# Sparse value rows fetched by SyncE at register addresses instead of GpSimd's indirect gathers

## The chip, the cores and the metric

The kernel runs on one core of a Trainium2 chip. A core has TensorE (PE in the profile; its weight loads are PEld), VectorE (DVE), ScalarE (ACT), GpSimd (POOL) and SyncE (SP), which each run one list of instructions in order and wait for each other on semaphores. Sixteen DMA engines move data between memory and the core; SP, ACT and POOL can issue transfers to them. The metric is the device time of one execution in microseconds: before the change the median of three runs is 290.01 (289.61 to 290.08).

## The reference

Attention of 4 batches with 8 heads, 768 positions and head dimension 64, with a block-sparse mask of 32 x 32 blocks (24 blocks a side), then a gated feed-forward layer on the 3072 x 512 result:

```python
scores = scale * np.matmul(q, k.transpose(0, 1, 3, 2))
mask = np.abs(blk_i - blk_j) <= 1
mask = mask | (blk_i == 0) | (blk_j == 0) | (blk_i == n_blocks - 1) | (blk_j == n_blocks - 1)
for qb in range(n_blocks):
    for kb in sampled_blocks[qb]:          # three per query block, drawn at random
        mask[qb * block:(qb + 1) * block, kb * block:(kb + 1) * block] = True
scores = np.where(mask, scores, -1000000000.0)
attn = softmax(scores)
x = (attn @ v) as (3072, 512)
rms = np.sqrt(np.mean(x * x, axis=-1, keepdims=True) + 1e-06)
xn = x / rms * rms_g
g = xn @ w_gate
silu = g * (1.0 / (1.0 + np.exp(-g)))
out = (silu * (xn @ w_val)) @ w_out
```

So a query block in the middle sees eight key blocks: its own and its two neighbours, the first, the last, and up to three sampled ones, which can coincide with the others or with each other.

## The kernel before

Batch 0 is computed densely, with the mask added in the score product: three groups of 256 positions (`groups`), eight heads each. While this runs, the kernel prepares the sparse part. Batches 1 to 3 are cut into 18 *chunks* of four query blocks (`chunks`, lines 70 to 75): five regular ones per batch, and one "wide" chunk with blocks 0, 23, 1 and 22, of which the first two see every key. The wide chunks are numbers 5, 11 and 16.

Each key or value block of 32 positions is held as 16 rows, two positions side by side. So the eight blocks that a query block sees fill exactly 128 partitions: three sampled blocks in partitions 0 to 47 (from `R0`), the first block in 48 to 63 (`F0`), the window of three in 64 to 111 (`W0`), the last in 112 to 127 (`L0`).

The values of a batch are cast to bfloat16 (`cast_v`), written to a table in memory (`table`, 384 rows of 1056 elements, that is 2112 bytes, with 16 rows of zeros behind them, `zero_rows`), and fetched from it. `gather_v` (line 508) issues for each query block one indirect transfer on GpSimd that fetches 128 rows of the table by 128 row numbers, a column of `vidx`, into a buffer `vgs[i % 2][:, j, :]`. `vidx` is built once: constant parts by `iotas`, sampled rows by DVE in `index_steps`, which sends a sampled block that repeats another block to the zero rows. There are 66 gathers: four for each of 15 regular chunks, two for each of three wide ones.

The loop over the chunks (line 1078) runs 19 steps of ten positions. In step `i` PE computes the scores of chunk `i` and, at position 0, the values product of chunk `i-1` (`values`, line 634, matmuls of L644), which reads that chunk's buffer. Position 1 and 2 normalise it, 4 squares it on ACT, 5 takes the power on GpSimd, and at position 7 DVE scales it (`x_scaled`, line 688) and SP sends a transposing transfer of it into `xg` (line 700); chunks 4, 8, 16 and 17 are transposed by PE instead (`by_pe`). At position 2, step `i` issues the gathers for chunk `i+1`. The first gathers, of chunks 0 and 1, are issued in the last dense group.

The feed-forward layer runs as *pieces* between these: groups of chunks (`sgroups`: 0 and 1; 2 to 4; 5 to 8; 9 to 12; 13 to 15; 16 and 17) enter the list of pieces two steps after their last chunk, at position 4, and `position` hands them out evenly until the next group enters. A group starts with `gate(0)` (L737), which reads the whole `xg` of the group; `val` is L748, `down` L766, and ACT copies a finished tile of the result to one of three `yo` buffers (L771), which SP stores (L717, L726).

SP's list holds 76 instructions in the order in which the program wrote them: loads of the first heads, copies of the mask rows, loads of raw V (L138), the zero rows (L442), the stores and the transposing transfers. Each of its transfers takes the next of eight semaphores and waits for the transfer eight places before it.

Of the kernel before, what the change touches and what calls it, by code (L numbers as in the profile page):

```python
# [18 lines left out]
def kernel(  # L19
# [12 lines left out]
    nc = tc.nc  # L32
    P = 128
# [13 lines left out]
    NT = S // 2  # L47
# [308 lines left out]
    qb = const.tile([NS, NB], FP32, name="qb")  # L356
    rs = const.tile([NS, NB, NRND], FP32, name="rs")
    pp_i = const.tile([NS, 1], I32, name="pp_i")
    pp = const.tile([NS, 1], FP32, name="pp")
    good = const.tile([NS, NB, NRND], FP32, name="good")  # L360
    tmp = const.tile([NS, NB, NRND], FP32, name="tmp")
    eps = const.tile([P, 1], FP32, name="eps")

    def iotas():
        def iota(t, lo, hi, cols, step, base, per=1):
            nc.gpsimd.iota(t[lo:hi, cols], pattern=[[step, cols.stop - cols.start]], base=base,
                           channel_multiplier=per)

        every = slice(0, NB)
        iota(p_i, 0, P, slice(0, 1), 0, 0)  # L370
        iota(qb_i, 0, NS, every, 1, 0, 0)
        iota(vidx, F0 - HB, W0, every, 0, -HB)
        iota(vidx, F0 - HB, W0, slice(1, 2), 0, NT - HB)
        iota(vidx, L0 - HB, P, every, 0, NT - 2 * HB)
        iota(vidx, L0 - HB, P, slice(NB - 2, NB - 1), 0, NT - HB)
        iota(vidx, W0, W0 + 32, every, HB, -HB)
        iota(vidx, W0 + 32, L0, every, HB, HB)

# [3 lines left out]


    def index_steps():
        yield lambda: nc.vector.tensor_copy(out=qb, in_=qb_i)
        yield lambda: nc.vector.tensor_copy(out=rs, in_=samp)
        yield lambda: nc.vector.tensor_scalar(out=pp_i, in0=p_i[0:NS], scalar1=HB - 1, scalar2=None,
                                              op0=ALU.bitwise_and)
        yield lambda: nc.vector.tensor_scalar(out=pp, in0=pp_i, scalar1=float(NT), scalar2=None,
                                              op0=ALU.add)  # L390
        yield lambda: nc.vector.tensor_tensor(out=tmp, in0=rs,
                                              in1=qb.unsqueeze(2).to_broadcast([NS, NB, NRND]),
                                              op=ALU.subtract)
# [7 lines left out]
        for step in range(1, NRND):  # L401
# [19 lines left out]
    def address(c, r, n=1):  # L421
        eng = ET.Activation if by_act(c, r) else ET.Pool
        _, vals = nc.values_load_multi_w_load_instructions(
            kofs[0:1, r * NB + c:r * NB + c + n], engines=[eng], min_val=0, max_val=NT - HB,
            skip_runtime_bounds_check_because="a sampled block is one of the sequence's")
        for m, x in enumerate(vals):
            kat[(c + m, r)] = x

    by_need = [(x, r) for i in range(PB) for x in chunks[i][1] if x not in (0, NB - 1)
# [29 lines left out]

    def spaced(ap, step, n, width):
# [44 lines left out]

    def gather_v(i, js=range(QB)):
        b, qbs = chunks[i]
        for j in js:  # L510
            if qbs[j] not in (0, NB - 1):
                nc.gpsimd.indirect_dma_start(  # L512
                    vgs[i % 2][:, j, :], None, vtab[b][:],
                    bass.IndirectOffsetOnAxis(ap=vidx[:, qbs[j]:qbs[j] + 1], axis=0))

# [91 lines left out]
    def bursts(i):  # L607
        return 8 if chunks[i][1][0] == 0 else 4

# [24 lines left out]
    def values(i, g):  # L634
# [3 lines left out]
        ops.setdefault(i, []).append(op)  # L638
        vg = vgs[i % 2].rearrange("p j (w h x) -> p j w h x", w=2, h=H)
        per = H // bursts(i)  # L640
# [209 lines left out]
    def side_work(gi, h):  # L850
# [23 lines left out]
        if gi == 2:  # L874
# [16 lines left out]
            if h > 3:  # L891
                load_v(2, h - 4)
            if h == 5:
                gather_v(0)
# [4 lines left out]
            if h == 7:  # L899
                gather_v(1, (0, 1))  # L900
                load_kq(2, 2)
# [176 lines left out]
    for i in range(NCH + 1):  # L1078
        jobs = {}

        def do(n, f):
            jobs.setdefault(n, []).append(f)
# [4 lines left out]
        if i == 0:  # L1087
# [7 lines left out]
            do(3, lambda: load_kq(2, 3))  # L1095
            do(7, lambda: gather_v(1, (2, 3)))
        else:
# [25 lines left out]
        if nx is not None:  # L1123
# [73 lines left out]
```

## Time and profile before

| what | value |
|---|---|
| median of three runs | 290.01 us |
| the profiled execution's own time | 290.28 us |
| its span | 288.5 us |
| PE / DVE / ACT / POOL busy | 273.9 / 216.7 / 198.2 / 146.7 us |
| granted clock | 1.00 throughout |
| bytes by GpSimd's queue / by SP's and ACT's | 32.60 / 14.18 MB |

The page of the profile gives the busy time of each engine, the same in slices, the DMA queues, the chain of work that ended last, and groups of equal instructions with their count, total, mean and the idle time ahead of them. A busy PE is not PE at its peak, as matmuls overlap. Time that a sequencer spends on issuing a transfer isn't counted as busy; rows of "SPq" show it.

### The profile page before, as it was taken

To read this page: it belongs to the slowest core of one execution; us is meant where nothing else is said; L and a number is where in the kernel's file an instruction comes from. 1 tells how busy PE (TensorE), PEld (TensorE's weight loads), DVE (VectorE), ACT (ScalarE), POOL (GpSimd) and SP (SyncE) were. 2 spreads that over 40 slices of the span, in tenths; PEclk is the share of its full clock that TensorE was granted. 3 is DMA by queue.
4 is the path that set the end of the run, shared out by engine and by line. 5 is a ranking of instruction groups with operands and counts; after the bars stand their busy time and mean duration, and the time that the engine had idled before them with its cause. 6 is when DMAs were issued, how large, how long until landed. Compare 5 with 4: busy or idle time off the path is not lost.

```text
span 288.5 us, 9875 instructions
## 1 busy us (share of the span) xinstructions
PE 273.9 (95%) x3840; PEld 185.3 (64%) x3871; DVE 216.7 (75%) x596; ACT 198.2 (69%) x467; POOL 146.7 (51%) x244
## 2 busy tenths in 40 slices
PE   8798999898999899799999999999999999999995
PEld 6586896687668678666665555545545556664783
DVE  7888889678979959966999578796499951784580
ACT  4896786588589789759989878577746484533331
POOL 8857244558487585787887627627723330101000
PEclk9999999999999999999999999999999999999999
DMA  7999999999885479898995845426932252000102
GB/s 133 287 214 201 206 207 268 290 229 315 168 232 125 142 205 287 173 222 259 250 170 154 280 122 154 101 73 186 204 115 77 59 168 77 36 2 36 75 1 73
DMA packets 37426, 47.44 MB, mean 164 GB/s; under 512 B 11184, under 2 KB 29380, under 8 KB 37380
## 3 DMA queue, kind: packets, MB, share of 16 engines
q0 software_dynamic: 21184, 32.60, 51.1%
q1 hardware_dynamic: 16132, 14.18, 17.2%
q8 instruction: 30, 0.49, 0.7%
q14 instruction: 16, 0.13, 0.1%
q10 hardware_dynamic: 64, 0.03, 0.0%
HBM read 46.45 MB, written 8.83 MB: 192 GB/s over the span
## 4 chain that ended last, share of the span: by engine, by line
PE 64%; DVE 16%; DMA 11%; issue 3%; POOL 3%; ACT 2%; DVEq 0%; ACTq 0%; POOLq 0%
PE yp L766 19%; PE gp L737 16%; PE vp L748 15%; PE st L620 5%; DMA gain<-in_moe_rms_g_dram 5%; DVE u L752 4%; DVE hps L756 4%; DMA qbf<-in_q_dram 4%; PE op L644 4%; DMA vraw<-in_v_dram 3%; PE tqk L455 2%; PE st L527 2%; DVE stage L670 1%; DVE xs L698 1%; PE op L536 1%
## 5 line engine op out<-in xcount | busy, mean ns | idle before, releaser
L512 POOL DMA_INDIRECT vg<-vtab,vidx x66 | 65.5, 992 | 45.2 <-PE op L644 27.1
L737 PE MATMUL gp<-xg,wg 128*128 128x256 bf16 (+2 forms) x426 | 80.2, 307 | 2.2 <-DVE stage L670 0.9
L748 PE MATMUL vp<-xg,wv 128*128 128x256 bf16 (+2 forms) x428 | 80.0, 307 | 1.4 <-DVE u L752 0.6
L741 ACT ACTIVATE th<-gp 128x256 bf16<-128x256 f32 (+2 forms) x108 | 49.8, 463 | 37.6 <-PE gp L737 34.4
L752 DVE SCALAR_TENSOR_TENSOR u<-th,gp 128x256 bf16<-128x256 bf16 (+2 forms) x108 | 54.5, 504 | 22.1 <-ACT th L741 21.5
L766 PE MATMUL yp<-wo,hps 128*128 128x512 bf16 (+1 forms) x282 | 69.1, 370 | 1.6 <-issue 0.3
L756 DVE TENSOR_TENSOR hps<-u,vp 128x256 bf16<-128x256 bf16 (+2 forms) x108 | 55.1, 510 | 11.6 <-PE vp L748 0.5
L628 ACT ACTIVATE ex<-st 128x512 bf16<-128x512 f32 x84 | 50.4, 600 | 13.8 <-PE st L620 12.6
L737 PEld LDWEIGHTS <-wg 128*128 128x128 bf16 x432 | 39.7, 98 | 20.0 <-issue 2.0
L748 PEld LDWEIGHTS <-wv 128*128 128x128 bf16 x432 | 39.5, 98 | 18.6 <-issue 1.5
L766 PEld LDWEIGHTS <-hps 128*128 128x128 bf16 x300 | 26.1, 98 | 20.8 <-DMA wo<-in_moe_w_out_dram 0.3
L530 ACT ACTIVATE ex<-st 128x768 bf16<-128x768 f32 x42 | 33.3, 813 | 5.8 <-PE st L527 5.6
L771 ACT ACTIVATE yo<-yp 128x512 f32<-128x512 f32 (+1 forms) x25 | 14.6, 582 | 19.7 <-PE yp L766 19.5
L681 POOL TENSOR_TENSOR ssq<-ssq,eps 128x1 f32<-128x1 f32 x18 | 4.3, 241 | 39.6 <-ACT junk L677 38.1
L527 PE MATMUL st<-wide_q,wide_k 88*128 88x256 bf16 x144 | 22.9, 272 | 1.5 <-DVE wide_q L345 1.1
L644 PEld LDWEIGHTS <-ex 128*32 128x32 bf16 x1344 | 13.6, 95 | 7.8 <-issue 7.8
L670 DVE TENSOR_TENSOR stage<-op,rz 128x256 bf16<-128x256 f32 x36 | 15.3, 425 | 1.2
L644 PE MATMUL op<-vg,ex 128*32 128x66 bf16 x1056 | 15.2, 195 | 1.0 <-DVE u L752 1.0
L527 PEld LDWEIGHTS <-wide_k 88*128 88x128 bf16 x144 | 13.0, 97 | 5.0 <-DVE wide_q L345 2.0
L620 PEld LDWEIGHTS <-kg 128*128 128x128 bf16 x272 | 12.7, 98 | 5.2 <-issue 0.3
L620 PEld LDWEIGHTS <-wide_q 128*128 128x128 bf16 x256 | 12.5, 98 | 5.3 <-issue 0.2
L620 PE MATMUL st<-wide_q 128*128 128x64 bf16 x256 | 15.1, 193 | 0.1
(147 smaller groups left out, 379.6 us busy)
## 6 DMA issues: line engine op xcount, KB each, us to landing
out_dram<-yo SPq DMA_DIRECT2D x20, 256.0 KB
vraw<-in_v_dram SPq DMA_DIRECT2D x12, 384.0 KB
kbf<-in_k_dram POOLq DMA_DIRECT2D x15, 192.0 KB, 5.7
vtab<-Vs POOLq DMA_DIRECT2D x3, 792.0 KB, 6.2
qbf<-in_q_dram POOLq DMA_DIRECT2D x12, 192.0 KB, 8.4
vraw<-in_v_dram POOLq DMA_DIRECT2D x4, 384.0 KB, 6.4
wg<-in_moe_w_gate_dram POOLq DMA_DIRECT2D x4, 384.0 KB, 10.6
wv<-in_moe_w_val_dram POOLq DMA_DIRECT2D x4, 384.0 KB
```

The costliest lines, as they stand in the source:

```text
L512: nc.gpsimd.indirect_dma_start(vgs[i % 2][:, j, :], None, vtab[b][:], bass.IndirectOffsetOnAxis(ap=vidx[:, qbs[j]:qbs[j] + 1], axis=0))
L527: nc.tensor.matmul(out=at[:, e], lhsT=KT0[0:KR, h, jt * P:(jt + 1) * P], rhs=QT0[0:KR, h, c0 * P:(c0 + 2) * P], start=True, stop=True)
L530: nc.scalar.activation(out=ex[:, 3 * part:3 * (part + 1), :], in_=at[:, 0:3], func=AF.Exp, scale=SCALE)
L620: nc.tensor.matmul(out=st[:, at:at + UN], lhsT=lhsT, rhs=Qd[i % 2][:, h, :, :, j * HB:(j + 1) * HB].rearrange("p a w s -> p (a w) s"), sta ...
L628: nc.scalar.activation(out=ex.rearrange("p (u s w) -> p u s w", s=HB, w=2), in_=st.rearrange("p (u w s) -> p u s w", s=HB, w=2), func=AF.E ...
L644: nc.tensor.matmul(out=op[j * BLK:(j + 1) * BLK, at:at + VW], lhsT=lhsT, rhs=rhs, start=(n == 0), stop=(n == of - 1))
L737: nc.tensor.matmul(out=gp[:, 0:tg], lhsT=wg[:, c, f * P:(f + 1) * P], rhs=xg[:, c, 0:tg], start=(c == 0), stop=(c == KD - 1))
L741: nc.scalar.activation(out=th[:, 0:tg], in_=gp[:, 0:tg], func=AF.Tanh, scale=0.5)
L748: nc.tensor.matmul(out=vp[:, 0:tg], lhsT=wv[:, c, f * P:(f + 1) * P], rhs=xg[:, c, 0:tg], start=(c == 0), stop=(c == KD - 1))
L752: nc.vector.scalar_tensor_tensor(out=u[:, 0:tg], in0=th[:, 0:tg], scalar=1.0, in1=gp[:, 0:tg], op0=ALU.add, op1=ALU.mult)
L756: nc.vector.tensor_tensor(out=hps[f][:, 0:tg], in0=u[:, 0:tg], in1=vp[:, 0:tg], op=ALU.mult)
L766: nc.tensor.matmul(out=yp, lhsT=hps[f][:, tt * P:(tt + 1) * P], rhs=wo[:, f, lo:hi], start=(f == 0), stop=(f == NF - 1))
```

## The change

The indirect gathers on GpSimd go away, and with them `vidx` and its constant parts. The values of a chunk are fetched by ordinary transfers that SP issues: one for the windows of all four query blocks, two for the first and the last block, copied to all four (only for the first three chunks of each batch: the buffers, now three in turn, keep those rows afterwards; in a wide chunk, a zero row block for each of two blocks), and three for each query block, one per sampled block, at an address that SP works out from a register. The three numbers of a query block are packed as five bits each into one integer (`vpack`), read into one register per query block (`table_blocks`, 22 registers), and taken apart by a shift and a mask before each transfer. The index arithmetic on DVE is done on one partition instead of 48.

The fetch for chunk `i+2` is issued at position 8 of step `i`, right after the transposing transfer of chunk `i-1`; before, the fetch for chunk `i+1` was issued at position 2. Chunks 0 and 1 are fetched whole in the last dense group.

All in all SP gets 240 more transfers (198 of one sampled block, 18 of windows, 24 of first, last or zero rows), 330 shift or mask operations, 198 fused register operations and six register loads, and its list grows to 715 instructions; GpSimd loses 66 gathers and seven of its eight iotas at that place.

```diff
-    p_i = const.tile([P, 1], I32, name="p_i")
-    qb_i = const.tile([NS, NB], I32, name="qb_i")
-    vidx = const.tile([P, NB], I32, name="vidx")
+    qb_i = const.tile([1, NB], I32, name="qb_i")
+    vpack = const.tile([1, NB], I32, name="vpack")
...
-        for r, lo, hi in ((1, 0, 2 * HB), (0, 0, HB), (2, 2 * HB, 3 * HB)):
-            yield lambda r=r, lo=lo, hi=hi: nc.vector.tensor_scalar(
-                out=vidx[lo:hi], in0=tmp[lo:hi, :, r], scalar1=float(HB), scalar2=pp[lo:hi],
+        for r in range(NRND - 2, -1, -1):
+            yield lambda r=r: nc.vector.scalar_tensor_tensor(
+                out=tmp[:, :, r], in0=tmp[:, :, r + 1], scalar=32.0, in1=tmp[:, :, r],
                 op0=ALU.mult, op1=ALU.add)
+        yield lambda: nc.vector.tensor_scalar(
+            out=vpack, in0=tmp[:, :, 0], scalar1=float(sum(NB * 32 ** r for r in range(NRND))),
+            scalar2=None, op0=ALU.add)
...
+    def table_blocks(lo, hi):
+        _, vals = nc.values_load_multi_w_load_instructions(
+            vpack[0:1, lo:hi], engines=[ET.SP], min_val=0, max_val=32 ** NRND - 1,
+            skip_runtime_bounds_check_because="three numbers of five bits")
+        for m, x in enumerate(vals):
+            vat[lo + m] = x
+
+    def table_row(c, r):
+        at = nc.s_assert_within(
+            (vat[c] >> (5 * r)) & 31, 0, NB,
+            skip_runtime_bounds_check_because="a sampled block, or the zeros behind the table")
+        return at * HB
...
-    def gather_v(i, js=range(QB)):
-        b, qbs = chunks[i]
-        for j in js:
-            if qbs[j] not in (0, NB - 1):
-                nc.gpsimd.indirect_dma_start(
-                    vgs[i % 2][:, j, :], None, vtab[b][:],
-                    bass.IndirectOffsetOnAxis(ap=vidx[:, qbs[j]:qbs[j] + 1], axis=0))
+    def fixed_v(i):
+        b, qbs = chunks[i]
+        vg, t = vgs[i % 3], vtab[b]
+        if i % PB < 3 or wide(i):
+            for to, at, none in ((F0, 0, 1), (L0, NT - HB, NB - 2)):
+                if i % PB < 3:
+                    yield lambda to=to, at=at: nc.sync.dma_start(
+                        out=vg[to:to + HB],
+                        in_=t[at:at + HB, :].unsqueeze(1).to_broadcast([HB, QB, 2 * HV]))
+                else:
+                    j = qbs.index(none)
+                    yield lambda to=to, j=j: nc.sync.dma_start(
+                        out=vg[to:to + HB, j, :], in_=t[NT:NT + HB, :])
+        j0 = 2 if wide(i) else 0
+        step = (qbs[j0 + 1] - qbs[j0]) * HB
+        w = t[(qbs[j0] - 1) * HB:(qbs[j0] + 2) * HB, :]
+        yield lambda: nc.sync.dma_start(
+            out=vg[W0:W0 + 3 * HB, j0:QB, :],
+            in_=_dc.replace(w.unsqueeze(1), ap=[w.ap[0], [step * 2 * HV, QB - j0], w.ap[1]]))
+
+    def sampled_v(i, j):
+        b, qbs = chunks[i]
+        if qbs[j] in (0, NB - 1):
+            return
+        for r in range(NRND):
+            nc.sync.dma_start(out=vgs[i % 3][R0 + r * HB:R0 + (r + 1) * HB, j, :],
+                              in_=vtab[b][bass.ds(table_row(qbs[j], r), HB), :])
+
+    def gather_v(i):
+        for x in fixed_v(i):
+            x()
+        for j in range(QB):
+            sampled_v(i, j)
...
+            if h in (3, 4):
+                lo, hi = (1, NB // 2) if h == 3 else (NB // 2, NB - 1)
+                for c in range(lo, hi, 4):
+                    table_blocks(c, min(c + 4, hi))
             if h == 5:
                 gather_v(0)
...
             if h == 7:
-                gather_v(1, (0, 1))
+                gather_v(1)
...
-            do(7, lambda: gather_v(1, (2, 3)))
...
-            if nx > 1:
-                do(2, lambda: gather_v(nx))
+            if nx + 1 < NCH:
+                do(8, lambda: gather_v(nx + 1))
```

More of the change, by code (lines that the diff above doesn't have):

```diff
@@ L351 @@
     samp = samp_i.rearrange("p (a r w) -> p a r w", r=NRND, w=2)[:, :, :, 0]
-    p_i = const.tile([P, 1], I32, name="p_i")
-    qb_i = const.tile([NS, NB], I32, name="qb_i")
-    vidx = const.tile([P, NB], I32, name="vidx")
+    qb_i = const.tile([1, NB], I32, name="qb_i")
     kofs = const.tile([1, NB * NRND], I32, name="kofs")
[L356 to L361, printed above, removed]
+    vpack = const.tile([1, NB], I32, name="vpack")
+    qb = const.tile([1, NB], FP32, name="qb")
+    rs = const.tile([1, NB, NRND], FP32, name="rs")
+    good = const.tile([1, NB, NRND], FP32, name="good")
+    tmp = const.tile([1, NB, NRND], FP32, name="tmp")
     eps = const.tile([P, 1], FP32, name="eps")
     def iotas():
[L365 to L377, printed above, removed]
+        nc.gpsimd.iota(qb_i, pattern=[[1, NB]], base=0, channel_multiplier=0)
     def offsets():
@@ L458, in turn, with wide @@
             "p e (s c) -> p e s c", c=HC), in_=t.rearrange("p e c s -> p e s c"))
+    def wide(i):
+        return chunks[i][1][0] == 0
     def spaced(ap, step, n, width):
@@ L607, in bursts @@
     def bursts(i):
-        return 8 if chunks[i][1][0] == 0 else 4
+        return 8 if wide(i) else 4
     def scores(i, part):
@@ L638, in values @@
         ops.setdefault(i, []).append(op)
-        vg = vgs[i % 2].rearrange("p j (w h x) -> p j w h x", w=2, h=H)
+        vg = vgs[i % 3].rearrange("p j (w h x) -> p j w h x", w=2, h=H)
         per = H // bursts(i)
```

9 lines of the change are left out of this document (3 added, 6 removed).

## The prediction

> **What bounds the kernel now.** I read the page's engine shares first, then its chain that ended last and its costliest groups. (SP is SyncE in the profile, SPq what its sequencer issues.)
>
> ```profile
> span 288.5 us, 9875 instructions
> ...
> PE 273.9 (95%) x3840; PEld 185.3 (64%) x3871; DVE 216.7 (75%) x596; ACT 198.2 (69%) x467; POOL 146.7 (51%) x244
> ...
> PE 64%; DVE 16%; DMA 11%; issue 3%; POOL 3%; ACT 2%; DVEq 0%; ACTq 0%; POOLq 0%
> ...
> L512 POOL DMA_INDIRECT vg<-vtab,vidx x66 | 65.5, 992 | 45.2 <-PE op L644 27.1 <-issue 8.2 <-PE st L620 3.3
> ```
>
> TensorE is busy for 95% of the span and holds 64% of the chain. GpSimd, which the change relieves, holds 3%. Its 66 gathers are 65.5 of its 146.7 us, and the time in front of them is mostly GpSimd waiting for a free buffer, not somebody waiting for GpSimd.
>
> Next the same by stretch (columns: length, busy us of PE, PEld, DVE, ACT, POOL, clock, DMA share, GB/s), and from the chain in order of time the values matmuls that open a chunk's step, with the first gate of the fourth sparse group:
>
> ```profile
> 62.80:90.30 27.50, 25.86 (x360) 19.99 (x362) 23.08 (x71) 22.12 (x61) 20.27 (x35) 1.00 0.90 234
> 90.30:162.40 72.10, 68.68 (x1254) 48.40 (x1263) 58.03 (x157) 61.72 (x166) 52.58 (x84) 1.00 0.81 200
> 162.40:201.90 39.50, 38.88 (x626) 22.26 (x635) 31.44 (x73) 28.56 (x75) 21.24 (x36) 1.00 0.50 146
> 201.90:254.00 52.10, 51.47 (x696) 28.60 (x705) 34.51 (x76) 30.71 (x73) 14.84 (x27) 1.00 0.38 103
> ```
>
> ```profile
> 90.32 0.64 PE op L644 x64
> ...
> 162.38 0.62 PE op L644 x64
> ...
> 205.95 0.65 PE yp L766 x3
> ...
> 206.83 0.86 PE gp L737 x4
> ...
> 213.74 0.74 PE op L644 x64
> ...
> 226.74 0.64 PE op L644 x64
> ...
> 239.06 1.55 PE op L644 x128
> ```
>
> From 90.32 (values of chunk 1) to 162.38 (chunk 9) are eight steps, 9.0 us each; later ones take 13.0 (213.74 to 226.74) and 12.3 us. PE idles 3.4 us in the second stretch and 0.6 in each later one: no more than that can be won there. At 206.83 PE goes from a down-projection straight into the first gate of chunks 9 to 12: nothing is waited for there today.
>
> Last, SP's queue: start, length, instruction; then duration rows (ns min/median/max).
>
> ```profile
> 62.76 0.39 SPq L138 DMA_DIRECT2D vraw<-in_v_dram  x1
> 108.88 2.33 SPq L700 DMA_TRANSPOSE xg<-xs  x1
> 111.31 1.46 SPq L138 DMA_DIRECT2D vraw<-in_v_dram  x1
> 194.53 1.19 SPq L700 DMA_TRANSPOSE xg<-xs  x1
> 197.38 1.77 SPq L726 DMA_DIRECT2D out_dram<-yo  x4
> 201.85 1.20 SPq L700 DMA_TRANSPOSE xg<-xs  x1
> ```
>
> ```profile
> L726 SPq DMA_DIRECT2D out_dram<-yo x28: 330/352/454, 127.2 to 285.6; - x28
> L700 SPq DMA_TRANSPOSE xg<-xs x14: 1189/1196/2332, 91.3 to 234.7; - x14
> L442 SPq DMA_DIRECT2D vtab<-idle x3: 583/590/662, 43.1 to 44.5; - x3
> L485 POOLq FUSED_REGOPS  x3: 37/37/37, 96.7 to 96.9; - x3
> ```
>
> SP issues a transfer in about 0.35 us and, of four back to back, one per 1.77 / 4 = 0.44. It is idle most of the time today. That is the resource the change spends.
>
> **The change, part by part.**
>
> *Taken from GpSimd*: 66 gathers (65.5 us) and seven small iotas. Who gains? Two rows: who waits for its power step, and DVE's copies (mean 352 in the group row; 274/291/544 min/median/max).
>
> ```profile
> DVE xs L698 <- POOL rstd L682: 2.5, 2, 2.4
> ```
>
> ```profile
> L500 DVE COPY wide_q<-QN 64x512 bf16<-64x512 bf16 x20 | 7.0, 352 | 0.3
> ```
>
> ```profile
> L500 DVE COPY wide_q<-QN x20: 274/291/544, 79.8 to 233.5; 64x512 bf16<-64x512 bf16 x20
> ```
>
> If these 20 copies fell to their median they would save 20 x 0.061 = 1.2 us of DVE, which is on the chain for 16%. With the 2.5 us of waits, at most 3.7 us; I take a gain of 1.0, since PE has 3.4 us of idle at most in the stretch where both lie. Lower end nothing.
>
> *Bytes*: a gather moves 128 rows of 2112 B, 66 of them 17.8 MB; the new transfers move 15.7 MB (6.7 sampled, 6.7 windows, 2.4 for rows of the first and last block). Costed at nothing either way.
>
> *Index arithmetic and table loads*: two DVE instructions fewer, six register loads on SP ahead of 62.76, where SP waits for buffers. Nothing, hidden by that wait.
>
> *Added on SP*: 240 transfers, of which 198 are sampled blocks of 16 rows at a register's address, each with 2.67 register operations on average (330 shifts and masks, 198 fused ones). The price of one sampled transfer, c: the transfer itself between 0.33 (shortest L726) and 0.59 (median L442, the only transfer of SP that touches the value table); I take the 0.44 of the four stores, nearest because they too follow each other. The register operations: three fused ones started within 96.7 to 96.9, so 0.10 apart, 0.037 long. Bounds 2.67 x 0.037 = 0.10 and 2.67 x 0.10 = 0.27; I take 0.10 + 1.67 x 0.07 = 0.22 (full pitch for the fused one, middle for the rest). c = 0.66, ends 0.43 and 0.86.
>
> *Does SP fit?* Everything on SP is in one order: the transposing transfer of chunk i-1, then the values of chunk i+2, then whatever is stored or loaded. The values wait for a table (chunks 0, 6, 12) and for a buffer that chunk i-1 has left, both early; behind them stand the next stores (three yo buffers, ACT waits), the loads of raw V, and the next transposing transfer, for which a gate on PE waits. So I add up SP from the end of the load at 62.76 (63.15) to the transposing transfer of chunk 12, at 201.85 before: 138.7 us to fill. In it then lie 13 regular chunks of 12 sampled transfers and two wide ones of 6, 168 c; 15 windows and 22 edge or zero transfers at 0.44, 16.3; 11 transposing at 1.20, 13.2; 6 loads at 0.39, 2.3; 14 stores at 0.44, 6.2. That is 168 c + 38.0, and SP is full at c = 0.60. At 0.66 it is 148.9, so chunk 12's transpose is issued 10.2 us late.
>
> *Slack there*: 206.83 - 201.85 = 4.98 us from issue to the gate. What a landing needs I bound by GpSimd's gathers:
>
> ```profile
> DMA to landing us min/median/max: 3.5/4.3/8.2
> ```
>
> At 3.5 the slack is 1.5 us (at 4.98 none). So 10.2 - 1.5 = 8.7 us on PE at that gate.
>
> *Back-pressure*: at 108.88 a transpose took 2.33 and the load behind it 1.46, against 1.20 and 0.39: 2.2 us on SP in one place, with the DMA share at 0.81. With a burst behind every transpose I expect this once more than today, +2.2; bounds 0 and, at every one of eight transposes of the busy stretch, 18. Each transfer also waits for the one eight before it (eight semaphores in turn): eight at 0.66 are 5.3 us, over the median landing of 4.3 but under the longest of 8.2, so a little of this is in that bound too.
>
> *After that gate* steps are 12 to 13 us and SP needs 12 x 0.66 + 1.3 + 1.2 + a few stores = 11: no second loss. The values of a chunk have 22 of 30 positions, about 20 us, from issue to use; SP's burst takes 9 and a landing 4.3, so up to that gate they are not what breaks first.
>
> *Sum*, against the profiled execution's own 290.28 us (span 288.5, 1.8 around it; 0.3 above the median of 290.01): 290.3 + 8.7 + 2.2 - 1.0 = 300.2. **I predict 300 us.**
>
> A rule against the change: the Trainium skill, DMA: Bandwidth & Descriptors, section "Rules for kernel authors", says to coalesce many small transfers, since under 64 KB one pays mostly overhead. Here a 264 KB gather becomes up to 15 transfers, the sampled ones 33 KB each. The four stores of 64 KB at 0.44 each agree; no run here shows 33 KB.
>
> **Rivals.**
>
> *SP is not full, but the order costs a little* (c at most 0.60). Chunk 11's transpose ends at 195.72; behind it stand 15 transfers (12 x 0.60 + 3 x 0.44 = 8.5) and five stores (2.2): chunk 12's leaves at 206.4, 4.6 late, 3.1 beyond the slack. 290.3 + 3.1 - 1.0 = 292.4. For it: only c decides. Against it: it needs the register operations at their lower bound or cheaper transfers.
>
> *Issue time is hidden.* With c = 0.43: 195.72 + 12 x 0.43 + 3 x 0.35 + 2.2 = 204.1, 2.3 late, 0.8 beyond the slack; with the gain of 1.0 that is 290.1, no change. The Trainium skill, DMA: Bandwidth & Descriptors, section "Issuing engines are not separate DMA queues", would have it so: issuing from several engines only saves sequencer time, "which is usually small relative to the DMA itself". Against it by the rows: 0.44 of issue for 64 KB, of which the 200 GB/s of the table move 88 KB in that time.
>
> *Faster: GpSimd was holding the step back.* From c below 0.37 on (195.72 + 12 x 0.37 + 1.05 + 2.2 = 203.4) chunk 12's transpose is within the slack, and the gain counts alone: 1.0 to 3.7 us, 286.6 to 289.3. For it: POOL is busy 52.58 of 72.10 us between 90.3 and 162.4, with most of PE's idle there. Against it: the 3% of POOL on the chain, and c must lie under its lower bound, or the gain be most of the 3.7.
>
> *Table transfers at 0.59*: c = 0.81 with the same register cost; SP is 35 us late, and the time is about 325.
>
> **How the numbers follow.** SP paces the kernel: 0.60, spread over 294 to 314 (c up to 0.74); c beyond that 0.04; order alone, 290.7 to 294: 0.16; hidden 0.06; faster 0.14. What differs from no change by under 0.2% (0.6 us) can't be told from it here. So faster 0.14, same 0.06, slower 0.80. The range of 289.6 to 314 leaves out the faster case and the tail, 0.18; the likeliest case's own range is 294 to 314.
>
> **What would show it.** In SP's queue the sampled transfers should start about 0.66 apart, with hardly a pause from 63 to about 210, and chunk 12's transpose at 212 instead of 201.85. PE should stand before the first gate of chunks 9 to 12 for several us, with a DMA into xg as the releaser; the chain should then carry that DMA. POOL busy should fall to about 81, and the L500 copies towards 0.29. If the pitch is under 0.60 and SP pauses before its transposes, the forecast falls; if PE stands at values (L644) for vg instead, the place was wrong though SP was right; if it stands in steps before 160, the lateness came earlier than the sum says.

## The result, and the profile after

| kernel | time, median (range) | span of the profiled execution | TensorE's granted clock |
|---|---|---|---|
| before | 289.97 us (289.61 to 290.08, 4 runs) | 288.5 us | 1.00 |
| after | 332.61 us (332.31 to 334.21, 4 runs) | 330.8 us | 0.952 |

The ratio is 1.1484 (95% interval 1.1446 to 1.1522): slower, as forecast, but by 42.6 us and not by 10, and far outside the range.

The page of the kernel after: engine shares, the granted clock in 40 slices (tenths), the chain by engine.

```profile
span 330.8 us, 10823 instructions
...
PE 283.6 (86%) x3840; PEld 190.9 (58%) x3871; DVE 215.1 (65%) x594; ACT 199.7 (60%) x467; POOL 79.5 (24%) x171
...
PEclk9999999999979969997978999999957999999999
...
PE 55%; DMA 18%; SPq 10%; DVE 8%; issue 5%; POOL 3%; ACT 1%; DVEq 0%; ACTq 0%; POOLq 0%
```

POOL fell from 146.7 to 79.5, and SP's queue, which had no place on the chain, now holds 10% of it, the transfers it issues most of another 18%. PE was idle for 288.5 - 273.9 = 14.6 us before and is for 330.8 - 283.6 = 47.2 now: 32.6 of the 42.3 us. The other 9.7 us are PE being busy longer with the same 3840 matmuls. The same kernel by stretch (length, busy us of PE, PEld, DVE, ACT, POOL, clock, DMA share, GB/s) shows where that is:

```profile
62.80:90.30 27.50, 24.74 (x336) 18.96 (x335) 23.49 (x73) 21.21 (x59) 7.55 (x19) 1.00 0.81 169
90.30:120.00 29.70, 18.43 (x285) 13.16 (x285) 12.44 (x36) 14.91 (x39) 3.62 (x11) 0.86 0.65 141
120.00:150.00 30.00, 28.51 (x544) 21.19 (x544) 22.53 (x67) 23.66 (x65) 10.12 (x23) 0.97 0.74 143
150.00:180.00 30.00, 20.49 (x301) 13.48 (x304) 18.95 (x44) 17.93 (x46) 6.08 (x16) 0.88 0.77 152
180.00:210.00 30.00, 28.05 (x423) 16.52 (x424) 18.50 (x48) 21.46 (x53) 4.94 (x15) 0.95 0.54 137
210.00:240.00 30.00, 24.99 (x443) 14.15 (x447) 18.62 (x45) 16.61 (x46) 5.06 (x14) 1.00 0.67 114
240.00:270.00 30.00, 23.18 (x243) 11.05 (x248) 17.41 (x35) 12.61 (x30) 2.89 (x10) 0.83 0.39 97
```

Three stretches stand out, from 90, 150 and 240 us: PE idles 7 to 11 us in each, and in the same three its granted clock is down to 0.83 to 0.88. Before, every stretch showed 1.00.

What PE waits for (us in all, times, longest):

```profile
PE gp L770 <- DMA xg<-xs: 18.2, 2, 10.4
PE op L677 <- DMA vg<-vtab: 14.4, 11, 2.7
```

Two waits at a gate for a transposing transfer (7.8 and 10.4 us), and eleven short ones of the values matmuls (L644 before, L677 now) for the new transfers. Both kinds of transfer come from SP. Its queue in order of time:

```profile
64.69 11.75 SPq L540 DMA_DIRECT2D vg<-vtab  x12
...
80.19 12.51 SPq L540 DMA_DIRECT2D vg<-vtab  x12
...
106.05 8.87 SPq L540 DMA_DIRECT2D vg<-vtab  x12
115.02 1.20 SPq L733 DMA_TRANSPOSE xg<-xs  x1
...
139.43 10.52 SPq L540 DMA_DIRECT2D vg<-vtab  x12
...
233.06 8.52 SPq L540 DMA_DIRECT2D vg<-vtab  x12
241.67 2.24 SPq L759 DMA_DIRECT2D out_dram<-yo  x5
244.01 1.23 SPq L733 DMA_TRANSPOSE xg<-xs  x1
```

Bursts of 12 sampled transfers take 7.7 to 12.5 us. Chunk 1's transposing transfer leaves at 115.02 and chunk 12's at 244.01, not at 201.85; from 63 us to there SP always has a transfer to issue, or one that waits for an earlier one to land. The chain around those places, and where the values of chunks 2 and 9 open their steps:

```profile
104.76 0.89 PE op L677 x61
115.02 2.41 DMA xg<-xs
117.56 1.01 PE gp L770 x4
...
168.65 6.86 DMA vg<-vtab
...
191.16 0.66 PE op L677 x60
...
232.35 6.37 DMA vg<-vtab
244.01 2.39 DMA xg<-xs
246.45 1.89 PE gp L770 x4
```

From 104.76 to 191.16 are seven steps of 12.3 us, where a step took 9.0 before.

The rows of one sampled transfer on SP (ns min/median/max; the landing in us), and SP's waits for landings:

```profile
L540 SPq ALU_OP  x330: 32/37/51, 64.4 to 277.1; - x165
L540 SPq FUSED_REGOPS  x198: 46/46/60, 64.5 to 277.2; - x198
L540 SPq MOVE vg<-vtab x198: 29/29/39, 64.6 to 277.3; - x198
L540 SPq DMA_DIRECT2D vg<-vtab x198: 315/316/1567, 64.7 to 277.3; - x198
...
DMA to landing us min/median/max: 1.7/2.9/9.4
```

```profile
SPq L540 <- DMA vg<-vtab: 12.1, 13, 2.7
...
SPq L540 <- DMA vraw<-in_v_dram: 5.5, 3, 2.2
```

From these records, SP's time between 63.15 and 244.01 against the prediction's sum (us; the sums are over the single records):

```
                                predicted   measured
168 sampled transfers             110.9       133.4   (0.66 -> 0.794 each)
  register work and dispatch                   54.5   (0.32 each)
  issue, undisturbed (0.316)                   53.1
  held above 0.316                              7.9
  waits for landings                           17.9
windows, edge and zero rows        16.3        20.8
11 transposing transfers           13.2        14.6   (10: chunk 12's own issue is the end)
14 stores, 6 loads                  8.5        12.1
all                               148.9       180.9
```

Each measured term has the time from the end of the instruction before it on SP, so the terms add up to the whole.

### The profile page after: what moved, and what is told of

The parts are those of the page before. It is cut to its first block, busy times and chain, and to the rows that moved or that the text cites. A ratio compares the mean times of both kernels' runs of the same rounds, so it can differ in the third digit from the quotient of the medians.

```text
span 330.8 us, 10823 instructions
## 1 busy us (share of the span) xinstructions
PE 283.6 (86%) x3840; PEld 190.9 (58%) x3871; DVE 215.1 (65%) x594; ACT 199.7 (60%) x467; POOL 79.5 (24%) x171
## 3 DMA queue, kind: packets, MB, share of 16 engines
q1 hardware_dynamic: 27556, 30.22, 39.8%
## 4 chain that ended last, share of the span: by engine, by line
PE 55%; DMA 18%; SPq 10%; DVE 8%; issue 5%; POOL 3%; ACT 1%; DVEq 0%; ACTq 0%; POOLq 0%
PE vp L781 14%; DMA vg<-vtab 14%; PE gp L770 14%; PE yp L799 12%; SPq L540 7%; PE st L653 4%; PE op L677 3%; PE st L560 2%; DMA qbf<-in_q_dram 2%; PE op L569 2%; DVE hps L789 2%; DMA xg<-xs 1%; PE tqk L457 1%; DVE u L785 1%; SPq L520 1%
## 5 line engine op out<-in xcount | busy, mean ns | idle before, releaser
L770 PE MATMUL gp<-xg,wg 128*128 128x256 bf16 (+2 forms) x426 | 84.8, 321 | 20.7 <-DMA xg<-xs 18.2
L781 PE MATMUL vp<-xg,wv 128*128 128x256 bf16 (+2 forms) x428 | 82.8, 315 | 0.9 <-issue 0.2
L770 PEld LDWEIGHTS <-wg 128*128 128x128 bf16 x432 | 40.9, 101 | 40.7 <-issue 12.6
L789 DVE TENSOR_TENSOR hps<-u,vp 128x256 bf16<-128x256 bf16 (+2 forms) x108 | 55.1, 510 | 12.8 <-PE vp L781 2.1
L781 PEld LDWEIGHTS <-wv 128*128 128x128 bf16 x432 | 40.4, 100 | 19.4 <-issue 2.8
L804 ACT ACTIVATE yo<-yp 128x512 f32<-128x512 f32 (+1 forms) x25 | 14.6, 583 | 29.1 <-PE yp L799 20.1
L677 PE MATMUL op<-vg,ex 128*32 128x66 bf16 x1056 | 18.0, 202 | 14.9 <-DMA vg<-vtab 14.4
L677 PEld LDWEIGHTS <-ex 128*32 128x32 bf16 x1344 | 15.0, 99 | 22.5 <-DMA vg<-vtab 13.7
L702 DVE RECIPROCAL rz<-op 128x4 f32<-128x4 f32 x36 | 6.4, 176 | 18.1 <-PE op L677 18.0
L653 PEld LDWEIGHTS <-kg 128*128 128x128 bf16 x272 | 13.6, 102 | 5.9 <-issue 1.4
L653 PE MATMUL st<-Qd,kg 128*128 128x64 bf16 x272 | 15.4, 198 | 0.6 <-issue 0.6
```

The costliest lines, as they stand in the source:

```text
L653: nc.tensor.matmul(out=st[:, at:at + UN], lhsT=lhsT, rhs=Qd[i % 2][:, h, :, :, j * HB:(j + 1) * HB].rearrange("p a w s -> p (a w) s"), sta ...
L677: nc.tensor.matmul(out=op[j * BLK:(j + 1) * BLK, at:at + VW], lhsT=lhsT, rhs=rhs, start=(n == 0), stop=(n == of - 1))
L770: nc.tensor.matmul(out=gp[:, 0:tg], lhsT=wg[:, c, f * P:(f + 1) * P], rhs=xg[:, c, 0:tg], start=(c == 0), stop=(c == KD - 1))
L781: nc.tensor.matmul(out=vp[:, 0:tg], lhsT=wv[:, c, f * P:(f + 1) * P], rhs=xg[:, c, 0:tg], start=(c == 0), stop=(c == KD - 1))
L789: nc.vector.tensor_tensor(out=hps[f][:, 0:tg], in0=u[:, 0:tg], in1=vp[:, 0:tg], op=ALU.mult)
```

## The experiments

Names are those of the kernel after, and so are line numbers but for the runs that keep gathers. The letters stand for explanations that the expectations set against each other: A, the time that SP needs to issue; B, the waits for landings (a transfer waits for the one eight places before it); C, the transposing transfers that stand behind a burst; S, A and B together, as two limits one behind the other; T, the traffic in the DMA engines; U, a GpSimd that becomes late. Times that are compared with the kernel after are compared with its 332.61 us.

**The third block left out from chunk 3 on** (its rows keep what the buffer held).

```diff
-        for r in range(NRND):
+        for r in range(NRND if i < 3 else NRND - 1):
```

> The changed kernel, with the third sampled block of each query block not fetched from chunk 3 on (its rows keep old data). In the changed kernel SP issues without a pause from 63.0 to the transposing transfer of chunk 12 at 244.0 us, 181 us for what filled 138.7 before, and a sampled transfer took 0.79 us of it. Theory A (SP's sequencer time is the pace): 44 sampled transfers fewer before chunk 12's transpose, 44 x 0.79 = 35 us, so it leaves at about 209 and the kernel takes 293 to 300 us. Theory B (the pace is landing: eight semaphores, each waiting for the large window transfers): the windows are all still there, the kernel stays above 315. Theory C (the transposing transfers queued behind a burst are what costs): bursts shorten from 8.2 to 5.6 us, about 305 to 315.

306.86 us, ratio 1.0573 (1.0529 to 1.0618): above theory A's range, under B's and inside C's; the run without transposing transfers, below, speaks against C. The first gate of chunks 0 and 1 still starts 10.9 us late (115.88 against 105.01 in the kernel before), since chunks 0 to 2 are fetched whole; of the 17.1 us in the span only 6.2 are lost after it. Fewer transfers help much, and the early loss is one of its own.

**Fixed addresses** (other blocks are fetched than the drawn ones, and SP does no register work).

```diff
-                              in_=vtab[b][bass.ds(table_row(qbs[j], r), HB), :])
+                              in_=vtab[b][(qbs[j] + 5 * r + 3) % NB * HB:((qbs[j] + 5 * r + 3) % NB + 1) * HB, :])
```

> The changed kernel with the sampled blocks at addresses known when the program is built (a fixed pattern instead of the drawn one), so that SP has no shift, mask, fused or move operation; the same 240 transfers of the same sizes. In the changed kernel these operations take about 0.29 of the 0.79 us of a sampled transfer. Theory A: 168 x 0.29 = 49 us less before chunk 12's transpose, 132 of 138.7 us filled, 290 to 295 us. If transfers one behind the other pay what the register operations hid (0.44 each at the least, as the stores do): 168 x 0.5 + 47.6 = 131.6, the same. Theory B: nothing changes in the landings, above 320. Theory C: 305 to 315.

323.21 us, ratio 1.1136 (1.1066 to 1.1207). That is far over theory A's range and inside B's (above 320). The register work, 54 us of SP, is worth only 9 us of time. SP's waits in this run say why:

```profile
SPq L540 <- DMA vg<-vtab: 38.4, 29, 3.3
SPq L540 <- DMA vraw<-in_v_dram: 5.1, 6, 2.1
```

38.4 where it was 12.1: a transfer that is issued sooner waits longer for the one eight places before it. Theory A falls as the only cause.

**Windows, edge and zero rows issued by GpSimd** (same bytes, drawn blocks).

```diff
-                    yield lambda to=to, at=at: nc.sync.dma_start(
+                    yield lambda to=to, at=at: nc.gpsimd.dma_start(
```

> The changed kernel with the 42 transfers of windows and of first, last and zero rows issued by GpSimd; the 198 sampled ones stay on SP. Issue alone (theory A without the waits): SP loses 36 transfers and 21 us before chunk 12's transpose, 160 us remain, PE about 20 us late, 308 to 315 us. Theory B (SP's semaphore waits, some 17 us, come from sampled transfers waiting for a window transfer eight places before): these go too, 143 us remain, 293 to 298 us. GpSimd has the time (80 of 331 us busy).

324.83 us, ratio 1.1192 (1.113 to 1.1254): above both ranges. The waits for landings did not go, as B expected; up to chunk 12's transpose they are 23.0 us in all against 17.6. The slow landings behind which SP stands are now the loads of raw V:

```profile
SPq L540 <- DMA vraw<-in_v_dram: 16.1, 6, 5.7
...
SPq L540 <- DMA vg<-vtab: 4.4, 5, 1.6
```

**No transposing transfers** (PE transposes every chunk's rows).

```diff
-    by_pe = [*sgroups[-1], sgroups[1][-1], sgroups[2][-1]]
+    by_pe = list(range(NCH))
```

> The changed kernel with every sparse chunk transposed by PE (as chunks 4, 8, 16 and 17 are), so that no transposing transfer stands behind the value transfers. Theory A: SP loses 11 x 1.4 = 15.5 us before the values of chunk 14, 165 of 138.7 us remain; PE now waits only at the values matmuls (L677) for vg, and the kernel takes 312 to 322 us. Theory C: with the transposes gone the values have two steps of slack, 293 to 298 us. By theory B about 325.

317.98 us, ratio 1.0956 (1.0879 to 1.1033), as theory A had it and far over C's 293 to 298: the two gate waits are gone, and 28 us are still lost; PE's largest wait is now for the values. So the transposes behind the bursts are one place where SP's lateness comes out and not its source.

**The sampled transfers ahead of the fixed ones** (order alone).

```diff
-        for x in fixed_v(i):
-            x()
         for j in range(QB):
             sampled_v(i, j)
+        for x in fixed_v(i):
+            x()
```

> The same transfers, with each chunk's 12 sampled ones ahead of its window and edge rows. Theory S: the transfers that wait are those behind a slow landing (window and edge rows, 4.6 to 5.5 us); with these last, the wait falls on the next transposing transfer or the next burst's first ones, so SyncE's waits fall by half (17 to 8 us) and the time to 315 to 327. Rival (the sum of issue time alone sets the pace): within 2 us of 332.6. If the waits only move to the transposes: 330 to 338.

333.49 us, ratio 1.1488 (1.1319 to 1.1656): no change, and theory S's 315 to 327 missed. SP's waits for landings of raw V and values fell from 17.6 to 4.4 us, more than S asked for, and chunk 12's transpose leaves at 239.94 instead of 244.01. But the window now leaves last, and PE waits for it (from this run's view of line L531, who waited for it, us and times):

```profile
PE op L677: 13.8, 3
```

**Fixed transfers and the loads of raw V of the last two batches on GpSimd**, with the drawn blocks and then with fixed addresses (other blocks than drawn). The cut shows the loads; the fixed transfers and the addresses are changed as above.

```diff
-        (nc.sync if b else nc.gpsimd).dma_start(
+        (nc.sync if b == 1 else nc.gpsimd).dma_start(
```

> As the first of these three, but with the drawn blocks and their register operations on SyncE. Theory S: the landing limit is gone, what is left is 0.61 to 0.66 per sampled transfer, 12 in 7.6 us; the pace is then the one that the prediction priced, 0.65 x 168 and no back-pressure: 300 to 312. Rival (landing is the main thing, register work is hidden when nothing waits): 290 to 298. Rival T (the traffic itself): 315 to 325.

> Leaves out the sampled choice (fixed blocks instead of the drawn ones, no register operations on SyncE), and gives the windows, edge and zero rows and the raw V loads of the last two batches to GpSimd: both limits on SyncE are taken at once. Theory S (two limits in series, the register work and the landing of the transfer eight places before): SyncE's bursts of 12 shrink from 8-11 us to about 12 x 0.32 = 4 to 5 us, its waits for landings fall below 10 us in all, and the time is 290 to 302. Rival T (what costs is the traffic itself, 33 KB pieces fetched in bursts two chunks ahead, whoever issues it): 312 to 325, values still waited for by PE. Rival U (SyncE free, but GpSimd, which now issues 42 + 8 more, becomes late for power steps and casts): 303 to 312, with GpSimd as releaser on the chain.

With the register work 320.61 us, ratio 1.1044 (1.0919 to 1.1168), far over the 300 to 312 of theory S and in the range of rival T; without it 306.42, ratio 1.0555 (1.0456 to 1.0655), over S and in the range of rival U. U's sign is absent, though: GpSimd has 0% of that run's chain. Register work is worth 9 us with the fixed transfers on SP, and 14 with them on GpSimd. Neither run reaches the kernel before, and neither takes the waits for landings from SP: up to chunk 12's transpose they are 25.3 us in the first and 38.8 in the second. These are the second's:

```profile
SPq L540 <- DMA vg<-vtab: 20.5, 20, 3.2
...
SPq L540 <- DMA out_dram<-yo: 7.2, 5, 2.6
SPq L540 <- DMA xg<-xs: 6.6, 2, 4.5
```

The transfer eight places before is now a sampled one, a store or a transpose. So no run here shows what is left when SP neither works on registers nor waits. Of the 12.7 us that PE idles more in the second run than before, 8.0 lie in one stretch (the first row is its window, the second the landing of sampled transfers in it):

```profile
120.00:163.00 43.00, 33.86 (x578) 22.36 (x576) 30.53 (x79) 31.18 (x83) 22.77 (x50) 1.00 1.10 176
```

```profile
DMA to landing us min/median/max: 5.1/8.6/12.8
```

There the DMA engines' share is 1.10 (0.80 in the same stretch of the kernel after, 0.89 before), a 33 KB transfer lands in 8.6 us at the median, and eight of them in flight are one per 8.6 / 8 = 1.1 us. That SP's queue has become a queue in the DMA engines, as rival T has it, agrees with these rows for this stretch, where tables, raw loads and windows meet; no run tests it by itself.

**Half of each sampled row** (the second half of it is not fetched from chunk 3 on; the number of transfers is the same).

```diff
-            nc.sync.dma_start(out=vgs[i % 3][R0 + r * HB:R0 + (r + 1) * HB, j, :],
-                              in_=vtab[b][bass.ds(table_row(qbs[j], r), HB), :])
+            n = 2 * HV if i < 3 else HV
+            nc.sync.dma_start(out=vgs[i % 3][R0 + r * HB:R0 + (r + 1) * HB, j, 0:n],
+                              in_=vtab[b][bass.ds(table_row(qbs[j], r), HB), 0:n])
```

> The changed kernel with only the first half of each sampled row fetched from chunk 3 on (the same 198 transfers, 16.5 KB instead of 33 KB; the second half keeps what the buffer held). If landings are long because the bytes queue up on the DMA engines: fewer waits for the transfer eight places before, 318 to 326. If it is the count (issue and fixed part of a landing): 329 to 334.

329.99 us, ratio 1.1364 (1.1337 to 1.1392): 2.6 us for half the sampled bytes from chunk 3 on. It is the count of the sampled transfers and not their bytes.

**Late chunks, early chunks**: SP's transfers for chunks 9 to 17 only, or for 0 to 8 only, the others by gathers as before.

```diff
-            if nx > 1:
-                do(2, lambda: gather_v(nx))
+            if nx > 1 and not by_sp(nx):
+                do(2, lambda: gather_p(nx))
+            if nx + 1 < NCH and by_sp(nx + 1):
+                do(8, lambda: gather_v(nx + 1))
```

> Chunks 0 to 8 by GpSimd's indirect gathers as before, 9 to 17 by SyncE's transfers two chunks ahead. Theory S (SyncE is overfilled only where steps are 9 us and loads of raw V and tables run; later steps of 11 to 13 us hold a burst of 8 us): 288.5 to 293, hardly a wait of PE for values, the first gate of chunks 9 to 12 within 2 us of its place. Rival (landings behind bursts cost anywhere, so each burst takes its share): half of the loss, 300 to 312.

> The converse: chunks 0 to 8 by SyncE's transfers, 9 to 17 by indirect gathers. Theory S: the whole early loss of the changed kernel up to the values of chunk 9 is here (27 us there), the gate of chunks 9 to 12 loses nothing more: 312 to 320. Rival (what the prediction summed up: the lateness comes out at the gate of chunks 9 to 12): 290 to 300. Rival (losses are not additive, since a late PE gives SyncE time): 300 to 312.

From chunk 9 on: 303.63 us, ratio 1.0459 (1.0443 to 1.0475). Up to chunk 8: 323.2, ratio 1.1131 (1.1092 to 1.1169), 32.7 us more than before and above all three ranges; nearly all of it is in place by the gate of chunks 9 to 12 (238.22 against 206.67 before). By theory S the late half should have been free; it costs 13, in the rival's range, but not for the rival's reason, the landings. Its queue on SP, one step after another (lines of this run's kernel):

```profile
178.26 1.25 SPq L767 DMA_TRANSPOSE xg<-xs  x1
...
181.33 8.25 SPq L574 DMA_DIRECT2D vg<-vtab  x12
189.68 2.02 SPq L767 DMA_TRANSPOSE xg<-xs  x1
...
202.44 1.21 SPq L767 DMA_TRANSPOSE xg<-xs  x1
...
213.55 2.24 SPq L793 DMA_DIRECT2D out_dram<-yo  x5
215.90 1.23 SPq L767 DMA_TRANSPOSE xg<-xs  x1
```

A step takes SP 11.4, 12.8 and 13.5 us, while PE needs 8.2 to 11.2 there (values at 171.99, 183.23, 194.35, 202.50 and 213.67 before): a queue that is full again, with five stores and a transpose late at the end, where PE stands 10.2 us before the gate of chunks 9 to 12 (218.45 against 206.67). There are hardly any waits for landings in it (1.8 us): here it is issue and register work almost alone.

**The lookahead alone**: the kernel before, with three buffers and its gathers two chunks ahead, in the third position of a step and then in the ninth.

```diff
-            if nx > 1:
-                do(2, lambda: gather_v(nx))
+            if nx + 1 < NCH:
+                do(8, lambda: gather_v(nx + 1))
```

> The kernel before with one part of the change alone: three value buffers in turn and the indirect gathers two chunks ahead (all of chunk 1 in the last dense group). Prediction's working: GpSimd's gathers are waited for by nobody, so 289.5 to 290.5, the same. A rival: GpSimd, which waited 27.1 us for PE in front of its gathers, reaches its power step earlier: 288 to 289.

> The kernel before with three buffers and the indirect gathers two chunks ahead, now issued at the ninth position of a step instead of the third. If the 4.4 us of the earlier form were GpSimd's wait for the next batch's table: 289.5 to 291, GpSimd's wait in front of a gather under 1.5 us. If they come from the third buffer, or from transfers that run at another time: 293 to 296 again.

In the third position 294.6 us, ratio 1.0142 (1.0119 to 1.0164); both expectations missed. In the ninth (the cut above) 290.4 us, ratio 1.0006 (0.9991 to 1.0021): no change. GpSimd's longest wait ahead of a gather, in the first and in the second of them (ns min/median/max):

```profile
L512 POOLq EVENT_SEMAPHORE  x57: 17/17/5796, 60.4 to 219.9; - x57
```

```profile
L512 POOLq EVENT_SEMAPHORE  x56: 17/17/2767, 61.0 to 223.0; - x56
```

5.8 us fell to 2.8 when the gather no longer follows the table that it reads. That agrees with this wait being the cause of the 4.4 us, but no single row carries all of it, and the cause is not shown. What matters here: at the position that the change uses, the third buffer and the lookahead cost nothing.

**How many transfers SP holds.** The runs so far leave open whether every sampled transfer has its price, or whether nothing is lost until SP is full. Only one of three sampled blocks, and two of three, from the first chunk on; the rest is not fetched, but for one transfer of fixed rows in each of chunks 0 to 2. The cut is that of one of three.

```diff
+        if i < 3 and j == QB - 1:
+            nc.sync.dma_start(out=vgs[i % 3][R0 + 1 * HB:R0 + NRND * HB],
+                              in_=vtab[b][0:2 * HB, :].unsqueeze(1).to_broadcast([2 * HB, QB, 2 * HV]))
-        for r in range(NRND):
+        for r in range(1):
```

> Only the first of the three sampled blocks is fetched; in chunks 0 to 2 one transfer of fixed rows fills the places of the other two, later chunks leave there what the buffer held. 66 sampled transfers are left. Theory S (the sum of what SyncE has to issue up to chunk 12's transpose decides): 56 x 0.79 + 47 = 91 us of 138.7, SyncE pauses before its transposes, 289 to 292. Rival (every sampled transfer costs its share, full queue or not): a third of the loss, 303 to 306.

> The same with two of three fetched from the first chunk on (132 sampled transfers). Theory S: 112 x 0.79 + 47 = 135.5 us of 138.7, just full, so what the earlier run with two of three from chunk 3 on lost beyond the gate of chunks 0 and 1 goes: 291 to 299. Rival (a share each): two thirds of the loss, 316 to 320.

One of three took 291.17 and 296.02 us, two of three 301.68 and 298.50. Beside these two the kernel before took 314.8 to 317.0 us and not its 290, which nothing on record explains, so a ratio to it says nothing here. I set the spans of their profiled executions, 289.4 and 299.9 us, against the 288.5 of the kernel before as profiled earlier; the other execution of each has 294.2 and 296.7. With one of three PE's granted clock is 1.00, PE has no row of waiting for values or transposes worth 0.5 us, and the gate of chunks 9 to 12 starts at 207.14, against 206.67 before. Sampled transfers up to chunk 12's transpose, and the loss in the span of the profiled execution:

```
 56 transfers    0.9 us
112             11.4
124             17.1   (the first experiment)
168             42.3   (the change)
```

10.5 us for the 56 from 56 to 112 (of which 6.3 at the gate of chunks 0 and 1, where a transfer of fixed rows is in the way too), 30.9 for the next 56. At a share each the loss would be 14.1 us at 56 and 28.2 at 112; all four executions lie far under that (0.9 and 5.7, 11.4 and 8.2). So it is a full queue and no price for each. The loss begins at fewer transfers than the sum said (11 us at 112, where 112 x 0.66 + 38.0 = 112 us left 27 of the 138.7 free), since SP is full early, in chunks 0 to 3, before it is full on the average.

## Why the prediction was wrong, step by step

*Direction and resource: right.* SP's in-order queue paces the kernel; it has hardly a pause from 63 us on; chunk 12's transpose is late, and PE stands before the first gate of chunks 9 to 12 with a transfer into xg as the releaser. With a third of the sampled transfers nearly all of the loss is gone.

*Price of a sampled transfer, c = 0.66: near where SP issues undisturbed, by luck.* 0.32 of register work and dispatch plus 0.316 of issue is 0.64, but both terms lie outside their bounds: the register work was put at 0.22, at most 0.27, and left out the move that each transfer also has (198 in the rows above); the issue was put at 0.44, at least 0.33. The two errors cancel. (Its sentence that no run shows 33 KB is wrong as well: the three transfers of its upper bound, L442, are 33.0 KB each.) Over the stretch a transfer took 0.794. Put into the prediction's own formula, 168 x 0.794 + 38.0 = 171.4, 32.7 over the 138.7 there were. With 9.5 more from the windows, transposes, stores and loads, taken too low though one transpose too many was counted, that gives 42.2 us, as measured (244.01 against 201.85): the sum is the right one, and its terms were too small.

*The step that failed is back-pressure, taken at +2.2 with an upper bound of 18, and with it the judgement on the eight semaphores ("a little of this is in that bound").* It compared eight pitches of 0.66, 5.3 us, with the landing of GpSimd's gathers, a median of 4.3. But what stands eight places ahead of a transfer that waits is seldom a sampled one: by the order of SP's issues, 10.0 us of the waits are behind a window, 5.6 behind a load of raw V, 1.8 behind copied edge rows, 0.9 behind a sampled transfer. The DMA view of the kernel after (KB each, median us to landing):

```profile
vg<-vtab SPq DMA_DIRECT2D x204, 33.0 KB, 2.8
vg<-vtab SPq DMA_DIRECT2D x15, 396.0 KB, 4.7
...
vraw<-in_v_dram SPq DMA_DIRECT2D x12, 384.0 KB, 8.3
```

In the waits of SP's queue that is 12.1 + 5.5 = 17.6 us, and transfers held in issue (below) add some 10 by chunk 12's transpose: together 28 where the forecast had 2.2 and its bound 18. This is the account of SP's records; what these 28 us cost in time no run shows by itself. With only 4.8 us of such waits (fixed transfers last) nothing was won, since PE then waited for the windows; with 38.8 us of them (the last of the runs with GpSimd) 26 us were won; and with one of three blocks SP waits 14.3 us and next to nothing is lost. So the waits cost only where SP has no pause to take them in, and taking work from SP turns into waits for landings again. Issue and landing bound SP one behind the other; the DMA engines may be a third bound.

*"The values are not what breaks first": wrong.* The 20 us of slack were counted from the place in the program, and SP reaches that place late as soon as it is full. The first gate (chunks 0 and 1) starts at 117.56 instead of 105.01, the values of chunks 6 to 9 lose some 15 us more, and the gate of chunks 9 to 12, with its own wait of 10.4, starts 39.8 us late in all. The sum took the stretch as a whole; by step the prediction's own prices leave no room: 12 x 0.66 + 0.44 + 1.20 = 9.6 us, before any store or load, in steps of 9.0. The prediction named this case: PE standing in steps before 160 means that the lateness came earlier than the sum says.

*"After that gate no second loss": right in the kernel after*, where the end is 42.3 us late, 2.5 more than the gate. Its reason, 11 us of SP work in steps of 12 to 13, was too low: the run from chunk 9 on shows 11.4 to 13.5, up to the gate.

*PE's clock was not in the sum.* All idle time was counted at its length; PE's longer busy time adds 9.7 us to the 32.6 of idle, three tenths on top.

*The gain on GpSimd and DVE: the signs came, the gain can't be seen.* POOL is busy for 79.5 us (81 forecast), and the copies (now L505) take 292 ns at the mean, near the 0.29 forecast. Behind a PE that waits for SP this won nothing that a row shows.

*The rivals.* Hidden issue fell clearly. The Trainium skill's sentence that sequencer time is "usually small relative to the DMA itself" (DMA: Bandwidth & Descriptors, "Issuing engines are not separate DMA queues") speaks of one transfer, and one has 0.64 us on SP beside a median landing of 2.9; the 168 of them still fill 107.6 us of SP. The rule on coalescing in the Trainium skill (same page, "Rules for kernel authors") is what the trace bears out: half the bytes save 2.6 us, and with a third of the transfers 0.9 us of the loss is left in the profiled execution. Table transfers at 0.59 gave the nearest time, 325, by luck: they issue in 0.32 to 0.42, and the waits bring the pitch near the 0.81 of that rival.

## What to carry to other kernels

An in-order issuing engine is to be budgeted like any other: its sum of issue times per step against the step, in the shortest steps first, and well under full, since waits and holds added a quarter to the undisturbed price here (0.794 against 0.64). Where a queue of transfers is limited by how many may be in flight, look at the slowest landings among them and not only at the median: here nearly all waits stood behind windows and raw loads. A burst that replaces one indirect transfer by twelve direct ones also delays everything that is issued behind it: here transposes, stores and loads.

## What the runs showed of the hardware

*Long issues go with code loads.* After 60 us, 17 transfers on SP took over 0.62 us to issue (a transposing one over 1.45), 0.2 more than the longest usual. Of these, 15 overlap one of the 16 KB or 8 KB packets of the two instruction queues in the DMA records, which cover about a sixth of that time; five of them (start and length in us):

```
issue on SP                    code load
106.72  1.41  sampled          106.25  1.52  16 KB
131.39  1.42  sampled          130.91  1.53  16 KB
136.71  1.51  edge rows        136.88  0.95  16 KB
162.68  1.84  store            162.74  1.65   8 KB
236.27  1.57  sampled          235.86  1.62  16 KB
```

The 15 exceed the usual length by some 14 us, 10 of them before chunk 12's transpose. Overlap alone does not make an issue long: 47 of the 294 issues after 60 us overlap a packet and 15 of these are long, against 2 of the other 247. The kernel before has nearly as many 16 KB loads (30; 31 after) and only three long issues, two of them beside a load; 12 of its issues overlap one. That the load is the cause is read from the coincidence; it was not tested by itself.

*The granted clock falls where PE idles.* Stretches with 7 to 11 us of idle show 0.83 to 0.88, those with 1.5 and 2.0 us 0.97 and 0.95; the one from 210 us has 5.0 us and 1.00, but 3.9 of them are the beginning of the second gate wait. The records of the clock in the kernel after show why the length of idle alone does not tell: between 6 us and the end the clock is 1.00 but for spells at one half, each of 3.4 us or two or three times that, from 94.4, 114.9, 152.5, 166.1, 179.8 and 241.2 us (30.7 us in all up to 251.5). Those from 114.9 (6.8 us) and 241.2 (10.2 us) begin some 5 us into the two gate waits and outlast them by 4 to 5 us, in which PE works at the lower clock. The Trainium skill (TensorE: Matmul & The Clock Gate, "HAM oscillation — how this bites in real kernels") states the rule as no idle gap over about 3.4 us; the gate waits of 7.8 and 10.4 us agree. The other four do not: they begin at the end of waits of the values, or just behind, that are 1.2 to 2.7 us long, so here shorter gaps went with a spell too.
